# Level-zero attention weights from row products on VectorE instead of tiled matmuls, and tile products kept together on TensorE

## The chip, the cores and the metric

The kernel runs on one core of one Trainium2 chip. The metric is device time in microseconds from launch to the last store, taken as the median over repeated executions. Five engines work side by side, each through its own queue in order: TensorE (matmuls, in the profile PE, with its weight loads as PEld), VectorE (DVE), ScalarE (ACT), GpSimd (POOL) and SyncE (SP, which here only starts transfers). They wait for each other through semaphores.

## The reference

An RWKV-6 attention block feeds an MLP-mixer block. All data is float32 (the four mixer weights are float64 on input and are converted by the kernel itself).

```python
# attention, B, H, S, D = 4, 8, 768, 48
for t in range(S):
    cur = einsum('bhd,bhe->bhde', u[None] * k[t], v[t])
    y[t] = einsum('bhd,bhde->bhe', r[t], state + cur)
    state = w[t][..., None] * state + einsum('bhd,bhe->bhde', k[t], v[t])
# mixer on x = y as (B, S, 384)
xt = x.transpose(0, 2, 1)
h = maximum(xt @ w_tok1, 0) @ w_tok2            # 768 -> 256 -> 768 tokens
uu = x + h.transpose(0, 2, 1)
out = uu + maximum(uu @ w_ch1, 0) @ w_ch2       # 384 -> 1536 -> 384 channels
```

Written without the loop, token t takes from an earlier token s the value v[s] with the weight sum over d of r[t,d] k[s,d] times the product of w over the tokens between them. Its own value has the weight sum over d of r[t,d] u[d] k[t,d]. Between neighbours (s = t-1) no w lies, and the weight is the plain dot product of r[t] and k[t-1].

## The kernel before

**Units.** The work on attention is cut into 12 units of 256 tokens (`NU`), three to a batch (`UB`), each of two chunks of 128 tokens (`UC`), each of two blocks of 64 (`T`). For a unit, r and k lie transposed: features of a pair of heads on the partitions, tokens along the row. Three sets of buffers (`rs`, `ks`, `ws`, `weights_at`) go round.

**Levels.** `levels(i)` fills unit i's 64 by 64 weight matrices in `weights_at` by doubling. At level l, blocks of 2^l tokens are joined: `gram(l)` (L256, and L250 for the last) forms products of k with the r of the neighbouring block on TensorE, in tiles of 64 by 64 or 32 by 32; `join(l)` (L288 to L290) then multiplies k, r and the running products of w on VectorE so that the next level can use them; `pick(l)` (L272 on VectorE, L267 and L280 on ScalarE) copies the wanted entries from PSUM into `weights_at` under a mask. Level 0 is apart. `begin` has ScalarE copy r and k into `rp` and `kp` with every second token multiplied by u (L217, L221). `gram0` (L233) multiplies these in 32 tile products for each unit, and `pick0` (L239) takes own-token and next-token entries.

**Posts.** `post(i)` is what turns the weights into outputs: `tokens` transposes k on TensorE (L323, copied out by ScalarE L324), `carry` forms the k-v products (L333), `update` the states on VectorE (L347, L350), `before` multiplies r by the carried state (L370) and `within` the weights by v (L383). Those three matmul groups use 64 by 64 tiles. Then unit i+3's r, k, w and v are requested on SP's queue.

**Mixing.** `mixing(bt)` is the mixer for one batch: `hidden` (L421), `back` (L428, and an addition on VectorE, L430), transposes (L440), `up` (L448, copied out by L450 on ScalarE), and `down`, in the form `quarters`: seven products (L482) on sums and differences made by VectorE (L474 to L477 and L492 to L520). These matmuls use the whole 128 by 128 array.

**Order.** Beside the mixing of batch bt stand the posts of batch bt+1, and beside post(i) the levels of unit i+1 (`beside`). `woven` merges the two lists by the costs written in them. Below that, the tile framework's scheduler sets the final order of each engine's queue, so the queues aren't simply the order of the calls; it also inserts the waits. PSUM has two `gram` buffers, one pair `a` used in turn by kv_ps and y_ps, and two `m` buffers for mixing; for batches after the first, the transposes of k use `m` too. The last batch's mixing has no attention beside it. The first batch's attention, and the conversion of the mixer weights on VectorE, stand at the start, before any mixing can fill TensorE.

Of the kernel before, what the change touches and what calls it, by code (L numbers as in the profile page):

```python
# [10 lines left out]
f32 = mybir.dt.float32  # L11
# [9 lines left out]
T = 64  # L21
# [33 lines left out]
def rwkv6_then_mixer(  # L55
    ctx: ExitStack,
    tc: tile.TileContext,
    rkw: bass.AP,
    v: bass.AP,
    u: bass.AP,  # L60
    w_tok1: bass.AP,
    w_tok2: bass.AP,
    w_ch1: bass.AP,
# [13 lines left out]

    nc = tc.nc
    pe, dve, act, pool, sp = nc.tensor, nc.vector, nc.scalar, nc.gpsimd, nc.sync

    const = ctx.enter_context(tc.tile_pool(name="const", bufs=1))
    wts = ctx.enter_context(tc.tile_pool(name="wts", bufs=1))
# [16 lines left out]
    def load_rkw(i):  # L99
        if i >= NU:  # L100
            return
        for n, t in enumerate((rs[i % 3], ks[i % 3], ws[i % 3])):
            for rows in (slice(0, 128),) if i < 3 else (slice(0, D), slice(P, P + D)):
                sp.dma_start(t[rows], rkw[i, n, rows, :])
# [7 lines left out]

    u_col = const.tile([128, A], f32, name="u_col")
    act.dma_start(u_col, u)
    load_rkw(0)
    load_rkw(1)

# [3 lines left out]
    for l in range(4):  # L121
        b = 1 << l
        m = const.tile([128, 64 // b, 2 if l == 0 else b], f32, name=f"mask{l}")
        pool.memset(m, 1.0)
        pool.affine_select(out=m, in_=m, compare_op=ALU.is_ge, fill=0.0, base=0,
                           pattern=[[-2 * b, 64 // b], [0, m.shape[2]]], channel_multiplier=1)
        pool.affine_select(out=m, in_=m, compare_op=ALU.is_ge, fill=0.0, base=b - 1,
                           pattern=[[2 * b, 64 // b], [1 if l == 0 else 0, m.shape[2]]], channel_multiplier=-1)
        n, x = (T, 1) if l == 0 else (32, UC * A)
        m8 = const.tile([128, x, n], u8, name=f"mask8_{l}")  # L130
        flat = m.rearrange("p n b -> p (n b)")
        for j in range(2):
            dve.tensor_copy(m8[ts(j, T)], flat[ts(j, T), ts(j, n)].unsqueeze(1).to_broadcast([T, x, n]))
        masks.append(m8)
# [62 lines left out]
    def levels(i):  # L197
# [7 lines left out]
        def begin():  # L205
            decay = apool.tile([128, COLS // 2], f32, name="decay")
            L["w"] = apool.tile([128, UC, A, 2], f32, name="w_chunk", bufs=4)
            pool.memset(L["w"], 0.0)
            products.extend([w_, decay, w_[:, :COLS // 4], decay[:, :COLS // 8], w_[:, :COLS // 16],
                             decay[:, :COLS // 32], L["w"].rearrange("p c a j -> p (c a j)")])  # L210

            rp = L["rp"] = apool.tile([128, COLS], f32, name="rp")
            kp = L["kp"] = apool.tile([128, COLS], f32, name="kp", bufs=1)
            both = [(t.rearrange("p (n two) -> p n two", two=2)[:ROWS], x.rearrange("p (n two) -> p n two", two=2)[:ROWS], o)
                    for t, x, o in ((rp, r_, 1), (kp, k_, 0))]
            for t, x, o in both:
                act.copy(t[:, :, o], x[:, :, o])  # L217
            for t, x, o in both:
                t, x = (e[:, :, 1 - o].rearrange("p (c a n) -> p c a n", c=UC, a=A) for e in (t, x))
                for a in range(A):  # L220
                    act.mul(t[:, :, a, :], x[:, :, a, :], u_col[:ROWS, a:a + 1])  # L221
# [78 lines left out]
            join(l, products[l], products[l + 1])  # L300
            pick(l)

        pieces = [(0.1, begin), (1.6, first_block)]
        for l in range(1, LEVELS):
            pieces.append((1.2, lambda l=l: block(l)))
        return pieces

    def post(i):
        bt, half = divmod(i, UB)
# [3 lines left out]
        def tokens():  # L313
            if half == 0:
                xs[bt] = xpool.tile([128, C, DM], f32, name="x")
            L = live[i]
            L["kT"] = apool.tile([128, UC, A, 128], f32, name="kT", bufs=1)
            if bt == 0:
                both = ps_g.tile([128, 2, 512], f32, name="gram").rearrange("p c (a t) -> p c a t", a=A)
            for c in range(UC):  # L320
                ps = both[:, c] if bt == 0 else ps_m.tile([128, A, 128], f32, name="kT_ps", tag="m")
                for a in range(A):
                    pe.transpose(ps[:, a, :], k_[:, ts(c * A + a, 128)], ident)  # L323
                act.copy(L["kT"][:, c], ps)  # L324
# [207 lines left out]
        downs = [first if (bt, s) == (0, 0) else quarters(s) for s in range(S // SEG)]  # L532
        return hiddens, turned, ups, downs

    def beside(after, ahead):

        tokens, carry, update, before, within, *loads = after
        begin, first, *rest = ahead

        def one(*pieces):  # L540
            return (sum(c for c, _ in pieces), lambda: emit(pieces))

        return [begin, tokens, one(carry, first), update, one(before, rest[0]), one(within, rest[1]), *loads, *rest[2:]]


    hiddens, turned, ups, downs = mixing(0)
# [16 lines left out]
    for bt in range(B):  # L563
# [11 lines left out]
                pieces += ups[s] + downs[s]  # L575
        n = (bt + 1) * UB
        if n < NU:
            att = levels(n) if bt == 0 else []
            for i in range(n, n + UB):
                att += beside(post(i), levels(i + 1)) if i + 1 < NU else post(i)  # L580
            emit(woven(att, pieces))
        else:
            emit(pieces)
# [29 lines left out]
```

## Time and profile before

| | us |
|---|---|
| median of 9 runs | 617.14 (616.83 to 619.69) |
| the profiled execution | 618.18 |
| its span, first to last instruction | 616.4 |
| TensorE matmuls busy | 589.0 |
| TensorE weight loads busy | 500.7 |
| VectorE busy | 341.5 |
| ScalarE busy | 201.6 |
| tile products of level 0 (L233), all 12 units | 22.5 busy, 768 matmuls |

Each float32 matmul of the program stands in the profile as two passes, so 384 products of L233 are 768 entries; transposes are one pass. In the chain of waits, an entry is the time between an instruction and the next on the path, and so the cost of a matmul in a stream; the duration in the list of groups is the latency of one matmul, which overlaps the next. The profile can be cut where the batches' mixing begins, at the first `hidden` matmul of each batch. There are an opening (to 134 us), a stage with the rest of batch 0's mixing (to 235.5), one with batch 1's (to 374), one with batch 2's (to 508), and a last one with batch 3's alone.

### The profile page before, as it was taken

The page shows a single profiled execution, that of the slowest core. Times are in us where ns is not written, and L with a number is a line of the kernel's source. Part 1 is how long each engine was busy: PE and PEld are TensorE (multiplying, and loading weights), DVE is VectorE, ACT ScalarE, POOL GpSimd, SP SyncE. Part 2 cuts the span into 40 slices and gives each one's busy share as a digit, 9 for nine tenths or more (in the row PEclk, how much of TensorE's full clock was granted, in tenths as well). Part 3 has the DMA queues.
Part 4 walks back from the last instruction along what each step waited for, and adds up shares of the span by engine and source line. Part 5 has one row for each costly group of instructions (what it writes and reads, how often), then busy time and mean ns, then how long its engine had stood idle before and what let it go on. Part 6 is the DMA issues. An engine that isn't in the chain of part 4 may idle for free.

```text
span 616.4 us, 19870 instructions
## 1 busy us (share of the span) xinstructions
PE 589.0 (96%) x8980; PEld 500.7 (81%) x8980; DVE 341.5 (55%) x743; ACT 201.6 (33%) x500; POOL 7.2 (1%) x32
## 2 busy tenths in 40 slices
PE   3879789999999999999999999999999999999997
PEld 2867567876888896789899896789899895898987
DVE  5879889998676783536464372616244341040403
ACT  7054555530444433433232422332211411302020
POOL 4000000000000000000000000000000000000000
PEclk9999779999999999999999999999999999999999
DMA  9235555620232112011112100000000000000000
GB/s 347 108 80 190 174 177 163 213 73 27 56 105 79 54 56 79 28 53 28 54 28 79 27 29 27 2 2 3 27 2 28 2 15 14 0 6 21 25 2 26
DMA packets 19380, 38.63 MB, mean 63 GB/s; under 512 B 2112, under 2 KB 12864, under 8 KB 19296
## 3 DMA queue, kind: packets, MB, share of 16 engines
q1 hardware_dynamic: 19152, 37.36, 19.0%
q8 instruction: 70, 1.15, 0.8%
q14 instruction: 14, 0.11, 0.1%
q10 hardware_dynamic: 144, 0.00, 0.0%
HBM read 32.64 MB, written 4.72 MB: 61 GB/s over the span
## 4 chain that ended last, share of the span: by engine, by line
PE 88%; DVE 6%; ACT 2%; DMA 2%; issue 2%; SPq 0%; DVEq 0%; ACTq 0%
PE z_ps L448 29%; PE q_ps L482 25%; PE gram L256 8%; PE h_ps L421 6%; PE h_ps L428 5%; PE h_ps L458 3%; PE kv_ps L333 2%; PE y_ps L383 2%; PE gram L233 2%; PE y_ps L370 2%; PE kT_ps L323 1%; DMA scratch<-in_w_ch_dram 1%; PE gram L250 1%; PE xT_ps L440 1%; DMA w<-in_rkw_dram 1%
## 5 line engine op out<-in xcount | busy, mean ns | idle before, releaser
L448 PE MATMUL z_ps<-xT,wch 128*128 128x256 f32 x864 | 195.9, 382 | 0.1
L448 PEld LDWEIGHTS z_ps<-xT,wch 128*128 128x128 f32 x864 | 161.1, 190 | 22.6 <-ACT z L450 1.0
L450 ACT ACTIVATE z<-z_ps 128x256 f32<-128x256 f32 x144 | 55.1, 382 | 156.6 <-PE z_ps L448 142.1
L482 PE MATMUL q_ps<-wch,z 128*128 128x192 f32 x528 | 93.7, 329 | 0.0
L482 PEld LDWEIGHTS q_ps<-wch,z 128*128 128x128 f32 x528 | 86.3, 190 | 1.3
L482 PE MATMUL q_ps<-scratch,z 128*128 128x192 f32 x396 | 71.1, 330 | 0.0
L256 PEld LDWEIGHTS gram<-r,k 48*64 48x64 f32 x3072 | 60.5, 156 | 11.6 <-issue 5.9
L256 PE MATMUL gram<-r,k 48*64 48x32 f32 x3072 | 65.6, 237 | 3.8 <-DVE at L272 1.9
L482 PEld LDWEIGHTS q_ps<-scratch,z 128*128 128x128 f32 x396 | 64.3, 190 | 0.9 <-ACT kT L324 0.2
L288 DVE TENSOR_TENSOR k<-k,decay 112x512 f32<-112x512 f32 x36 | 24.8, 690 | 49.1 <-PE gram L256 37.0
L474 DVE TENSOR_TENSOR z<-z 128x768 f32<-128x768 f32 x11 | 10.5, 957 | 63.2 <-ACT z L450 63.1
L288 DVE TENSOR_TENSOR k<-k,w 112x512 f32<-112x512 f32 x36 | 24.8, 690 | 36.7 <-PE gram L256 31.5
L421 PE MATMUL h_ps<-x,wtok 128*128 128x384 f32 x96 | 38.9, 557 | 1.7 <-ACT x L389 1.6
L350 DVE SCALAR_TENSOR_TENSOR state<-state,w_chunk,kv_ps 128x48 f32<-128x48 f32 x160 | 30.7, 256 | 17.5 <-PE kv_ps L333 17.5
L428 PE MATMUL h_ps<-h,wtok 128*128 128x384 f32 x96 | 35.5, 494 | 0.1
L233 PE MATMUL gram<-rp,kp 48*64 48x64 f32 x768 | 22.5, 248 | 10.7 <-ACT kp L221 7.9
L272 DVE COPY_PREDICATED at<-mask,gram 128x512 f32<-128x512 uint8 x36 | 32.3, 897 | 0.0
L421 PEld LDWEIGHTS h_ps<-x,wtok 128*128 128x128 f32 x96 | 19.9, 218 | 14.1 <-issue 2.9
L233 PEld LDWEIGHTS gram<-rp,kp 48*64 48x64 f32 x768 | 18.4, 154 | 15.3 <-ACT kp L221 10.3
L280 ACT COPY at<-gram 16x256 f32<-16x256 f32 x48 | 17.4, 364 | 37.2 <-PE gram L256 35.2
L430 DVE TENSOR_TENSOR x<-x,h_ps 128x384 f32<-128x384 f32 x24 | 13.3, 554 | 27.4 <-PE h_ps L428 27.0
L289 DVE TENSOR_TENSOR r<-r,w 112x512 f32<-112x512 f32 x36 | 24.6, 685 | 3.6 <-ACT rp L217 3.6
(80 smaller groups left out, 552.4 us busy)
## 6 DMA issues: line engine op xcount, KB each, us to landing
scratch<-in_w_ch_dram SPq DMA_DIRECT2D x10, 512.0 KB, 4.5
vt<-in_v_dram SPq DMA_DIRECT2D x12, 384.0 KB, 3.7
out_dram<-o SPq DMA_DIRECT2D x24, 192.0 KB, 1.9
x<-in_w_ch_dram SPq DMA_DIRECT2D x8, 512.0 KB, 4.5
w<-in_rkw_dram SPq DMA_DIRECT2D x18, 192.0 KB, 3.3
k<-in_rkw_dram SPq DMA_DIRECT2D x18, 192.0 KB, 3.2
r<-in_rkw_dram SPq DMA_DIRECT2D x18, 192.0 KB, 3.5
scratch<-in_w_tok_dram SPq DMA_DIRECT2D x4, 512.0 KB, 9.1
```

The lines of the kernel that those rows point to most:

```text
L233: pe.matmul(g[cols, q, ts(a, T)], L["kp"][rows, tokens], L["rp"][rows, tokens], start=True, stop=True)
L256: fours(lambda q, j, rows, cols: pe.matmul(g[cols, q, ts(ca, 32)], k_[rows, ds(ca * 128 + j * T, T)], right[rows, ts(2 * ca + j, 32 // b), ...
L272: dve.copy_predicated(out=dst, data=g.rearrange("p q (m b) -> p q m b", b=b), mask=masks[l].rearrange("p x t -> p (x t)").rearrange("p (m ...
L288: dve.tensor_mul(left, left, wv[:, :, 1].unsqueeze(2).to_broadcast([ROWS, n, b]))
L289: dve.tensor_mul(right, right, wv[:, :, 0].unsqueeze(2).to_broadcast([ROWS, n, b]))
L350: dve.scalar_tensor_tensor(new[:, a], state[bt, g][:, a], L["w"][:, c, a, j:j + 1], got[:, a], op0=ALU.mult, op1=ALU.add)
L421: pe.matmul(sums[i], wtok1[:, c, ts(i, 128)], xs[bt][:, c, :], start=(c == 0), stop=(c == C - 1))
L428: pe.matmul(ps, wtok2[:, i, ts(c, 128)], h1[:, i, :], start=(i == 0), stop=(i == DTOK // 128 - 1))
L448: pe.matmul(ps, wch1[:, m, ts(jt, 128)], xT[:, m, ts(s, SEG)], start=(m == 0), stop=(m == DM // 128 - 1))
L450: act.activation(zs[s][:, jt, :], ps, AF.Relu)
L458: pe.matmul(ps, zs[0][:, jt, ts(n, 128)], wch2[:, jt, :], start=(jt == 0), stop=(jt == NJ - 1))
L482: pe.matmul(ps, a[:, j, :], b[:, j, :], start=(j == 0), stop=(j == HJ - 1))
```

## The change

- For units 3 to 11 `gram0`, `pick0` and the copies into `rp` and `kp` are gone; `begin` does `join(0)` instead.
- Their level-0 weights come from VectorE (`nearest`). r, the r of the following token, and k are loaded once more with tokens on the partitions (`load_near`: four more transfers for each unit on SP's queue, two of 384 KB and two of 192 KB). `row` multiplies them for one chunk of 128 tokens and sums over each head's 48 features; `place` writes the sums under the mask into `weights_at`.
- In `late`, the first unit's `nearest` is ordered behind VectorE's and SP's newest instructions at that point; the order of the others is left to the scheduler.
- `beside` orders the products of unit i+1's level 1, 2 and 3 directly behind the tile products of `carry`, `before` and `within` of unit i, as one run in tiles.
- The transposes of k always use one `gram` buffer, and `begin` gets a larger cost in the weaving, so that mixing stands between the last gram and the transposes.

```diff
@@ levels(i), begin
+            if i >= UB:
+                join(0, products[0], products[1])
+                return
...
-        pieces = [(0.1, begin), (1.6, first_block)]
+        pieces = [(0.1, begin)] + ([(1.6, first_block)] if i < UB else [])
...
+    def load_near(i):
+        if i >= NU:
+            return
+        L = near_by[i] = [apool.tile([128, COLS], f32, name="kp", bufs=1)]
+        for c in range(UC):
+            t = apool.tile([128, COLS], f32, name="rp")
+            sp.dma_start(t[:, :2 * DM].rearrange("p (two e) -> p two e", two=2), near[i - UB, c, :, :2, :])
+            sp.dma_start(L[0][:, ts(c, DM)], near[i - UB, c, :, 2, :])
+            L.append(t)
...
+        def row(c):
+            k, t = near_by[i][0][:, ts(c, DM)], near_by[i][1 + c]
+            rr = t[:, :2 * DM].rearrange("p (two e) -> p two e", two=2)
+            if c == 0:
+                sums.append(apool.tile([128, UC, 2 * H], f32, name="sums"))
+            dve.tensor_mul(rr, rr, k.unsqueeze(1).to_broadcast([128, 2, DM]))
+            dve.tensor_mul(rr[:, 0], rr[:, 0], u_rows)
+            dve.tensor_reduce(out=sums[0][:, c], in_=t[:, :2 * DM].rearrange("p (h e) -> p h e", e=D),
+                              axis=mybir.AxisListType.X, op=ALU.add)
+        def place():
...
+            for q in range(2):
+                dve.tensor_copy(v[:, q, :, :, 0], own[:, q])
+                dve.scalar_tensor_tensor(v[:, q, :, :, 1], own[:, q], odd, later[:, q], op0=ALU.mult, op1=ALU.add)
+            dve.copy_predicated(
+                out=weights_at[i % 3].rearrange("p q x (m two) -> p (q x) m two", two=2),
+                data=two.rearrange("p q x two -> p (q x) two").unsqueeze(2).to_broadcast([128, 2 * UC * A, T // 2, 2]),
+                mask=masks[0].rearrange("p x (m two) -> p x m two", two=2).to_broadcast([128, 2 * UC * A, T // 2, 2]))
+        return [(0.3, lambda: row(0)), (0.3, lambda: row(1)), (0.2, lambda: (place(), load_near(i + 1)))]
...
@@ post(i), tokens
-            if bt == 0:
-                both = ps_g.tile([128, 2, 512], f32, name="gram").rearrange("p c (a t) -> p c a t", a=A)
+            both = ps_g.tile([128, 2, 512], f32, name="gram").rearrange("p c (a t) -> p c a t", a=A)
             for c in range(UC):
-                ps = both[:, c] if bt == 0 else ps_m.tile([128, A, 128], f32, name="kT_ps", tag="m")
+                ps = both[:, c]
...
@@ beside
+        def both(f, g):
+            behind = products(f)[-1].name
+            for ins in products(g):
+                tc.add_manual_dep(ins, behind, no_sync, reason="products in tiles together")
         def one(*pieces):
-            return (sum(c for c, _ in pieces), lambda: emit(pieces))
-        return [begin, tokens, one(carry, first), update, one(before, rest[0]), one(within, rest[1]), *loads, *rest[2:]]
+            return (sum(c for c, _ in pieces), lambda: both(*(f for _, f in pieces)))
+        return [(1.0, begin[1]), tokens, one(carry, rest[0]), update, one(before, rest[1]), row0, one(within, rest[2]),
+                *loads, row1, *rest[3:], place]
...
@@ main loop, batch 0
+                marks = {e: newest(e) for e in (sp, dve)}
+                late(marks, lambda: (sp.dma_start(u_rows, u_all), load_near(n)))
+                att += levels(n) + [(c, lambda f=f: late(marks, f)) for c, f in nearest(n)]
```

`near` and `u_all` are new arrays laid out by the host from r, k and u, copies without arithmetic; `odd` is a column with one on the odd partitions, made once from the level-0 mask.

## The prediction, made before the changed kernel ran

> **What bounds the kernel now.** I read the busy table by stage first, cut where each batch's mixing begins (start:end, length, then PE, PEld, DVE and ACT busy).
>
> ```profile
> 0.00:133.96 133.96, 110.99 (x2059) 90.16 (x2060) 115.89 (x255) 65.84 (x153) 6.66 (x27) 0.95 0.54 175
> 133.96:235.50 101.54, 100.53 (x2303) 83.26 (x2302) 77.00 (x163) 37.20 (x97) 0.34 (x3) 1.00 0.23 65
> 235.50:373.95 138.45, 138.45 (x2217) 119.51 (x2218) 69.67 (x154) 45.45 (x118) 0.22 (x2) 1.00 0.14 41
> 373.95:507.83 133.88, 133.78 (x1871) 115.40 (x1871) 54.00 (x127) 34.51 (x86) 0.00 (x0) 1.00 0.03 11
> 507.83:616.40 108.57, 105.23 (x534) 92.42 (x533) 24.90 (x46) 18.65 (x47) 0.00 (x0) 1.00 0.04 13
> ```
>
> From 134 us on TensorE has no idle time to speak of. VectorE has 24.5 us free in the second row (101.5 - 77.0), 69 and 80 us in the next two. The opening is VectorE's and the transfers'. Busy doesn't prove full speed, so I took prices from the chain of waits (start, length, what), where matmuls stand at the rate at which they follow each other:
>
> ```profile
> 440.70 1.08 PE kv_ps L333 x64
> 441.78 0.94 PE gram L233 x58
> 442.72 9.26 PE z_ps L448 x42
> 507.83 7.74 PE h_ps L421 x24
> 554.68 15.54 PE z_ps L448 x72
> 599.41 13.66 PE q_ps L482 x84
> ```
>
> A pass of L448 is 15.54 / 72 = 0.216 us, of L482 0.163, of a 384-wide product 0.323. A tile pass is about 0.0145, reached when a tile block follows another. A block of tiles behind whole-array work costs some 0.14 more (1.08 against 0.94), and the first whole-array block behind tiles 0.2 more (9.26 against 42 x 0.216 = 9.06). Transposes of k take 0.135, of x 0.11, the last gram's 32 by 32 tiles 0.009, all from the same view.
>
> With these prices and the order of the instructions, the four stages sum to 99.0, 137.2, 132.5 and 105.0 us; the trace has 101.5, 138.5, 133.9 and 105.2. So TensorE's own work is all but 5 us of the last 479, and that work is what a change must cut. The view of waits agrees; from 134 to 508 us it has one entry for matmuls:
>
> ```profile
> PE kT_ps L323 <- DVE k L288: 0.8, 2, 0.5
> ```
>
> [...] The 768-wide product measures 0.957, or 0.87 from start to start.
>
> **What the change takes away.** 32 products, 64 passes, for each of nine units. 512 of the 576 passes lie behind 134 us: 512 x 0.0145 = 7.4 us. The order of the instructions moves one more gram block (0.9) from the second stage into the opening, where TensorE has time. Tile products kept together, and transposes no longer mixed with level-0 products, cut the changes between tiles and whole array behind 134 us from 70 each way to 46: with the prices of each kind, 22.3 to 15.3 us, or 7.0. Together 15.3. By stage the sums are 89.9, 134.8, 128.9 and 105.0: less by 9.1, 2.4, 3.6 and 0.
>
> ScalarE loses 9 x (2 x 0.67 + 8 x 0.405) = 41 us of copies. It is 37 of 101 us busy in the fullest stage, so this is worth nothing directly. It can shorten the wait of the transposes for buffers; the 2.5 us between 99.0 and 101.5 bound that.
>
> **What it adds.** Nearest rows on VectorE (line, tiles, shape, count, busy and mean ns, idle before):
>
> ```profile
> L239 DVE COPY_PREDICATED at<-mask,gram 128x512 f32<-128x512 uint8 x24 | 17.2, 725 | 1.3 <-PE gram L233 1.2
> L474 DVE TENSOR_TENSOR z<-z 128x768 f32<-128x768 f32 x11 | 10.5, 957 | 63.2 <-ACT z L450 63.1
> L515 DVE TENSOR_TENSOR o<-o,z 128x384 f32<-128x384 f32 x11 | 6.1, 558 | 0.3
> ```
>
> Successive operations overlap by some 0.08 us (L288 takes 0.69 and the next starts 0.61 later), so I count from start to start. Each chunk: a 768-wide product 0.87, a 384-wide one 0.48, a reduce of 768. The reduce isn't in the trace: [...] 0.96 if like L474 without overlap; I take 0.86. Each unit also has four small operations, 0.1 each (L290 on 16 elements is 0.17 without overlap). The masked copy of 1024 is not there either. [...] the masked copy of level 1, whose runs are two elements long, takes twice as long as those of longer runs:
>
> ```profile
> 194.93 1.30 DVE L272 COPY_PREDICATED at<-mask,gram 128x512 f32<-128x512 uint8 x1
> 199.74 0.71 DVE L272 COPY_PREDICATED at<-mask,gram 128x512 f32<-128x512 uint8 x1
> ```
>
> The new copy reads 512 pairs, which at that price is 2 x 1.08 = 2.2. Its destination and mask run on without gaps, so I take 1.4. A unit costs 2 x 2.21 + 0.4 + 1.4 = 6.2, less two L239 copies, 1.2: about 5 us net, 45 over nine units.
>
> Spread evenly this hides under the 173 us that VectorE has free. It isn't spread evenly. In the order of the changed kernel, `late` holds back only the first unit; all others depend on their loads alone, and VectorE's queue in the second stage holds 12 of the 18 wide products, 11 narrow, 10 reduces, 10 pairs of small operations and 3 of 9 masked copies ahead of the operation that frees the PSUM buffer for batch 1's first matmul. That is 10.4 + 5.3 + 8.6 + 2.0 + 4.2 = 30.5 us. What else stands there, at start-to-start prices, is 64.6 (the 77.0 of before without six L239 copies, without one level of joins that moves into the opening, and without the last rows of the stage). VectorE starts 0.9 us after TensorE here, so even without a pause it reaches that operation at 0.9 + 95.1 = 96.0, where TensorE would be at 89.9. **In this stage VectorE becomes the bound.** It won't run without a pause, since joins still wait for grams; I add 2 us, an estimate between the 24.5 it was idle and none. The stage takes 98.0: 3.5 us less, not 9.1.
>
> What is late next: 13.2 us of VectorE work stand between that operation and the end of batch 1's first addition to x, for which the first transpose of x waits. TensorE has about 14 us of its own before it (the 12 products of `hidden`, two passes each, 0.645, the transposes of k, a tile run, the first products of `back`). I take 0.5 us. The third stage then gains 2.4 - 0.5 = 1.9. VectorE is about half busy from there, with 4 wide products left, and the fourth gains 3.6.
>
> **Transfers.** Four more issues a unit on SP, 0.38 us each, two of 384 KB (v's, the same size, land in 3.7 us) and two of 192 (3.3). Space for the next pair of rows is freed by a reduce, and between a reduce and the product that reuses its buffer lie 6.5 to 11 us of VectorE work: 0.4 + 3.7 fits, with 2.4 us to spare at the tightest. I take 1 us in all, and 5 or more as the bad case below. DMA engines are a quarter busy.
>
> **Opening.** Two L239 copies (1.2) leave VectorE, one level's join and pick (2.5) come in, where it idles 0.8 us for a transfer; the transposes ahead of SP's wait at 78 us come earlier. I take -0.3, from -1 to +1.
>
> **Sum.** -0.3 - 3.5 - 1.9 - 3.6 + 1.0 = -8.3 against the profiled span of 616.4 us (618.18 with what lies around it). The median of runs is 617.14, 1 us below that execution; taking the difference to it gives **609.0 us**.
>
> **Rivals.**
>
> 1. *TensorE stays the bound throughout*: the whole 15.3 arrives, near 603. For it speaks that TensorE was the bound everywhere. Against it stands the sum of VectorE's queue: [...].
> 2. *The unseen operations are dear*: masked copy 2.2, reduce 0.96. Then the second stage takes 3 x 0.8 + 10 x 0.1 = 3.4 more and 1 more in the next: 613.4.
> 3. *Slower: VectorE stands in line for late row loads.* SP takes its queue in order, and loads of r stand in it until `before` has read r:
>
> ```profile
> SPq L104 <- PE y_ps L370: 15.2, 2, 7.8
> ```
>
> That is 15.2 us in two waits in the second stage alone. A row load behind such a wait misses its 2.4 us, its product stops VectorE's queue with the joins behind it, and as VectorE is the bound there each us counts. It turns the gain into a loss from 8.3 us in all, 0.7 for each of 12 products. At 1 us each: 621. Against it: the rows run units ahead of need, and the loads go out between the waits.
>
> That the change doesn't do what it says (tile runs torn apart again by the scheduler) is ruled out by the order, where the 46 changes stand.
>
> **How the numbers follow.** Chances: the forecast 0.50 (its own range 605 to 613), rival 1 0.09, rival 2 0.22, rival 3 0.19. Leaving out half of rival 1 and most of rival 3's tail, the range is 604 to 619. A change of 0.2%, 1.2 us, is about what can be told from none. Faster: 0.50 + 0.09 + 0.16 of rival 2 = 0.75. The same: 0.05 of rival 2, 0.04 of rival 3. Slower: 0.01 and 0.15.
>
> **What will show it.** The second stage near 98 us with VectorE over 90 busy, and TensorE waiting there for VectorE some 6 to 9 us; 136.5 and 130 in the next two; the last unchanged. Runs of 128 tile passes, and no L233 group beyond the first three units. Prices of the reduce and the wide masked copy decide between the forecast and rival 2, idle time of the row products for transfers rival 3. The prediction fails if VectorE reads rows slower than the 768-wide row says, or if TensorE's switch prices aren't what the tile runs save.

## The result

The changed kernel takes 612.12 us, the median of 16 runs (607.82 to 615.18), against 617.0 for the kernel before beside it. The ratio is 0.992 (95% interval 0.9904 to 0.9937): faster by 0.8%. The forecast was 609.0 with a range from 604 to 619. The profiled execution took 612.79 us, with a span of 611.0; the span of before was 616.4.

The busy table of the changed kernel by stage, cut as in the prediction (start:end, length, PE, PEld, DVE, ACT and POOL busy, then the mean granted TensorE clock, the share of the DMA engines and GB/s):

```profile
0.00:132.90 132.90, 109.19 (x2059) 88.78 (x2060) 115.27 (x256) 56.65 (x128) 6.66 (x27) 0.88 0.58 187
132.90:237.40 104.50, 96.55 (x1946) 80.54 (x1945) 98.43 (x209) 23.94 (x61) 0.34 (x3) 0.95 0.41 117
237.40:373.13 135.73, 135.57 (x2128) 117.57 (x2128) 87.07 (x188) 36.98 (x93) 0.22 (x2) 1.00 0.23 69
373.13:502.51 129.38, 129.38 (x1743) 112.39 (x1743) 54.75 (x129) 32.48 (x81) 0.00 (x0) 1.00 0.03 11
502.51:611.00 108.49, 105.24 (x535) 92.52 (x533) 24.91 (x46) 18.60 (x47) 0.00 (x0) 1.00 0.04 13
```

Only the later cuts stand at a batch's first `hidden` product; the first stands at batch 0's first product of `down` (L458 before, L533 now).

| stage | before | after | change | forecast |
|---|---|---|---|---|
| opening | 133.96 | 132.90 | -1.1 | -0.3 |
| second | 101.54 | 104.50 | **+3.0** | -3.5, and +1.0 for transfers |
| third | 138.45 | 135.73 | -2.7 | -1.9 |
| fourth | 133.88 | 129.38 | -4.5 | -3.6 |
| last | 108.57 | 108.49 | -0.1 | 0 |
| sum | 616.40 | 611.00 | -5.4 | -8.3 |

So one stage went the other way. In the second row VectorE is busy 98.4 of 104.5 us, TensorE 96.6, and the clock column reads 0.95, where before it read 1.00. Neither engine is without a pause, and TensorE was not at full speed.

TensorE's longest waits from the second stage to the end of the fourth (line waited for: us in all, times, longest); the one entry of before was 0.8 us:

```profile
PE gram L289 <- DVE r L322: 3.4, 4, 1.2
PE gram L289 <- issue: 3.2, 2, 2.1
PE y_ps L445 <- DVE state L425: 0.9, 2, 0.7
```

TensorE now waits for the joins of VectorE (L322), and twice for nothing that the profile can name ("issue"). The chain of the fourth stage shows what the change did for TensorE where nothing disturbs it: `carry` and a gram block follow each other with one change to tiles, and the same rates hold as before.

```profile
439.73 1.08 PE kv_ps L408 x64
440.81 0.93 PE gram L289 x63
```

The new operations, which the trace of before couldn't price (groups: out<-in, shape, count, busy and mean ns, idle before):

```profile
L362 DVE TENSOR_TENSOR rp<-rp,kp 128x768 f32<-128x768 f32 x18 | 17.1, 952 | 1.1 <-DMA rp<-in_near_dram 1.1
L364 DVE TENSOR_REDUCE sums<-rp 128x16 f32<-128x768 f32 x18 | 17.0, 946 | 0.1
L375 DVE COPY_PREDICATED at<-mask,two 128x1024 f32<-128x1024 uint8 x9 | 11.8, 1310 | 1.0 <-ACT at L300 0.9
L363 DVE TENSOR_TENSOR rp<-rp,u_rows 128x384 f32<-128x384 f32 x18 | 9.9, 552 | 0.1
```

The reduce runs like the product of its width, 0.946 us against 0.952. The masked copy of 1024 takes 1.31 us, near the 1.4 taken and far from the 2.2 of rival 2. In the whole kernel the row products waited 1.1 us in all for their own loads.

The second stage's chain, in the middle (start, length, what), names two things that the forecast had not placed:

```profile
195.86 0.21 SPq L128
...
196.12 4.05 DMA r<-in_rkw_dram
...
200.26 0.69 DVE r L322
...
202.30 1.13 PE gram L289 x62
203.43 1.11 issue
...
204.96 3.71 PE z_ps L523 x8
```

A load of r, not of a row, came late: its two halves were issued at 195.69 and 196.12, VectorE waited 1.4 us for them, to 200.26, and TensorE got its gram at 202.30. Then TensorE stopped in the middle of its gram passes for 1.11 us with nothing to wait for. And 8 passes of L523 took 3.71 us, where 8 x 0.216 = 1.73 is their price.

### The profile page after: what moved, and what is told of

Same layout as the page of the kernel before. It is cut to its first block, busy times and chain, and to the rows that moved or that the text cites. A ratio compares the mean times of both kernels' runs of the same rounds, so it can differ in the third digit from the quotient of the medians.

```text
span 611.0 us, 18750 instructions
## 1 busy us (share of the span) xinstructions
PE 575.9 (94%) x8404; PEld 491.8 (80%) x8404; DVE 380.4 (62%) x826; ACT 168.6 (28%) x410; POOL 7.2 (1%) x32
## 3 DMA queue, kind: packets, MB, share of 16 engines
q8 instruction: 66, 1.08, 0.8%
## 4 chain that ended last, share of the span: by engine, by line
PE 74%; DVE 18%; issue 4%; ACT 2%; DMA 2%; SPq 0%; DVEq 0%; ACTq 0%
PE z_ps L523 24%; PE q_ps L557 23%; PE gram L289 6%; PE h_ps L496 6%; PE h_ps L503 5%; DVE r L322 2%; PE y_ps L458 2%; DVE k L321 2%; PE kv_ps L408 2%; PE y_ps L445 2%; DVE state L425 1%; PE gram L398 1%; DVE wch L205 1%; DVE at L305 1%; DVE rp L362 1%
## 5 line engine op out<-in xcount | busy, mean ns | idle before, releaser
L523 PE MATMUL z_ps<-xT,wch 128*128 128x256 f32 x864 | 197.9, 385 | 0.1
L523 PEld LDWEIGHTS z_ps<-xT,wch 128*128 128x128 f32 x864 | 162.6, 192 | 22.4 <-ACT z L525 1.4
L557 PE MATMUL q_ps<-wch,z 128*128 128x192 f32 x528 | 96.0, 333 | 0.0
L557 PEld LDWEIGHTS q_ps<-wch,z 128*128 128x128 f32 x528 | 88.1, 193 | 1.7 <-DVE o L579 0.3
L557 PE MATMUL q_ps<-scratch,z 128*128 128x192 f32 x396 | 70.3, 329 | 0.1
L557 PEld LDWEIGHTS q_ps<-scratch,z 128*128 128x128 f32 x396 | 64.4, 190 | 0.7 <-issue 0.3
L549 DVE TENSOR_TENSOR z<-z 128x768 f32<-128x768 f32 x11 | 10.5, 957 | 61.8 <-ACT z L525 61.8
L321 DVE TENSOR_TENSOR k<-k,decay 112x512 f32<-112x512 f32 x36 | 24.8, 688 | 31.3 <-PE gram L289 18.7
L321 DVE TENSOR_TENSOR k<-k,w 112x512 f32<-112x512 f32 x36 | 24.8, 689 | 30.2 <-PE gram L289 25.1
L322 DVE TENSOR_TENSOR r<-r,w 112x512 f32<-112x512 f32 x36 | 24.7, 686 | 4.7 <-DMA r<-in_rkw_dram 4.7
L322 DVE TENSOR_TENSOR r<-r,decay 112x512 f32<-112x512 f32 x36 | 24.6, 685 | 0.0
L503 PEld LDWEIGHTS h_ps<-h,wtok 128*128 128x128 f32 x96 | 16.9, 193 | 9.7 <-ACT h L498 2.5
```

Source lines behind the costliest of these rows:

```text
L321: dve.tensor_mul(left, left, wv[:, :, 1].unsqueeze(2).to_broadcast([ROWS, n, b]))
L322: dve.tensor_mul(right, right, wv[:, :, 0].unsqueeze(2).to_broadcast([ROWS, n, b]))
L503: pe.matmul(ps, wtok2[:, i, ts(c, 128)], h1[:, i, :], start=(i == 0), stop=(i == DTOK // 128 - 1))
L523: pe.matmul(ps, wch1[:, m, ts(jt, 128)], xT[:, m, ts(s, SEG)], start=(m == 0), stop=(m == DM // 128 - 1))
L557: pe.matmul(ps, a[:, j, :], b[:, j, :], start=(j == 0), stop=(j == HJ - 1))
```

## The experiments

Three theories stood against each other at first. **V**: VectorE's row operations, which only their loads hold back, run ahead and stand in VectorE's queue before the joins that TensorE waits for. **T**: TensorE's lower clock is the loss. **S**: the late loads of r are. All edits are to the changed kernel unless another is named.

| kernel | whole us (runs) | ratio to before, 95% | second stage | DVE busy in it | clock in it |
|---|---|---|---|---|---|
| after | 612.12 (16) | 0.992, 0.9904 to 0.9937 | 104.5 | 98.4 | 0.95 |
| e1_spread | 606.79 (5) | 0.9836, 0.981 to 0.9862 | 95.7 | 89.9 | 1.00 |
| e2_no_rows | 601.6 (5) | 0.9765, 0.9735 to 0.9796 | 93.9 | 75.4 | 1.00 |
| e3_together_only | 613.67 (12) | 0.9949, 0.9933 to 0.9965 | 100.3 | 75.0 | 1.00 |
| e4_near_only | 614.35 (20) | 0.9954, 0.9935 to 0.9972 | 102.7 | 102.4 | 0.99 |
| e5_loads_only | 611.47 (6) | 0.9912, 0.9877 to 0.9947 | 102.5 | 76.9 | 0.97 |
| e6_spread_apart | 604.47 (5) | 0.9802, 0.9777 to 0.9827 | 93.7 | 89.4 | 1.00 |
| e7_spread_pool | 610.98 (6) | 0.9903, 0.9867 to 0.994 | 100.7 | 87.7 | 0.98 |
| e8_short_loads | 607.07 (5) | 0.984, 0.9809 to 0.9871 | 98.4 | 97.5 | 1.00 |
| e9_loads_held | 604.02 (4) | 0.98, 0.9772 to 0.9827 | 95.7 | 76.0 | 1.00 |

Each ratio sets a kernel against executions of before that were taken with it. e2, e5, e8 and e9 leave out a part of the computation, as told below. The second stage is cut at the same two matmuls in all. The openings lie between 131.5 and 135.5 us and hide or add a little of it, so a length is read beside the whole time. In e2, e5, e8 and e9 the order puts one gram block of 64 passes (0.9 us) into this stage that the changed kernel, e1, e6 and e7 have in the third.

### Rows held at their place (e1)

```diff
-        row0, row1, place = nearest(i + 1)
+        row0, row1, place = ((c, lambda f=f: late({dve: newest(dve)}, f)) for c, f in nearest(i + 1))
```

Every unit's row operations now stay behind the operation that was VectorE's newest where their piece stands, not only the first unit's.

> Every row, sum and copy of the new VectorE work stays behind VectorE's newest instruction at its place in the list, so it no longer runs units ahead. TensorE's order stays nearly the same (its sums by stage: 89.9, 134.8, 128.9, 105.0 us). VectorE's work up to the operation that frees batch 1's first PSUM buffer falls from 94.5 to 85.8 us, below TensorE's 89.9. Theory V (VectorE's queue is what made the second stage long): that stage goes from 105.3 us to 92 to 96, and the whole to about 602 (600 to 605). Theory T (TensorE's granted clock, 0.80 in one stretch of that stage, made it long): the stage stays at 102 or more, the whole at 610 to 613. Theory S (late loads of r): the stage stays above 100 with VectorE waiting for transfers.

Measured 606.79 us, second stage 95.7. Nothing was taken away: the same operations, loads and tile runs, 8.8 us less in that stage. Only the order differs. The stage lies where V had put it and the clock in it was 1.00; the whole is 1.8 us above V's range, and the opening took 134.9, 2.0 more than in the changed kernel. At this point I took V for settled, and T and S for refuted: T had said 610 to 613, S a stage above 100. That was too quick, as e5 shows: holding the products also holds the loads that wait for their buffers, so e1 changes two things at once.

### Rows left out, and each half of the change alone (e2, e3, e4)

e2 leaves out the loads, products and sums of the rows, with constant weights in their place:

```diff
...
-            dve.tensor_mul(rr, rr, k.unsqueeze(1).to_broadcast([128, 2, DM]))
-            dve.tensor_mul(rr[:, 0], rr[:, 0], u_rows)
-            dve.tensor_reduce(out=sums[0][:, c], ...)
+                sums.append(flat_sums)
...
-        return [..., (0.2, lambda: (place(), load_near(i + 1)))]
+        return [..., (0.2, place)]
...
-                late(marks, lambda: (sp.dma_start(u_rows, u_all), load_near(n)))
```

> Leaves out part of the computation: the new loads, the row products and the sums; the level-0 weights of units 3 to 11 are placed from a constant. What is left of the change on VectorE is the small operations and the masked copy. TensorE's work and order as in the changed kernel. Theory V: the second stage is TensorE's again, 91 to 95 us, and the whole 599 to 603; this is the ceiling of what the change could give. Theory T: still 610 or so, with the clock low in the second stage. Theory S can't be told from V here, since loads and rows are both gone.

601.6 us, second stage 93.9: the ceiling, and close to the 603 of rival 1. Rows cost the changed kernel 10.5 us of the whole, nearly all of it in the second stage (104.5 - 93.9 = 10.6).

e3 keeps level 0 on TensorE for all units and takes only the other half: tile products together, transposes of k in the gram buffer.

```diff
-            if i >= UB:
-                join(0, products[0], products[1])
-                return
...
-        return [(1.0, begin[1]), tokens, one(carry, rest[0]), update, one(before, rest[1]), row0, one(within, rest[2]),
-                *loads, row1, *rest[3:], place]
+        return [(1.0, begin[1]), tokens, one(carry, first), update, one(before, rest[0]), one(within, rest[1]),
+                *loads, *rest[2:]]
...
```

> Level 0 stays on TensorE for all units, as before the change; tile products are ordered behind one another and the transposes of k use a gram buffer with mixing ahead of them. TensorE's sums by stage: 95.7, 137.7, 131.5, 105.0 us against 99.0, 137.2, 132.5, 105.0 before, all of it from fewer changes between tiles and whole array (109 against 139). If the price of such changes is right (0.14 to 0.2 us each): 3.8 us less than before, 613 to 614, second stage about 98. If they cost nothing by themselves: 617. Theory T adds: if longer runs of tile products lower the clock, the clock is below that of before, and the time is no better.

613.67 us, as expected: 15 of 70 changes to tiles and back fall away, which by the sums of the expectation is 3.8 us; the medians differ by 3.1 (0.0051 x 617). The second stage is 100.3 in the profiled execution, not the 98 expected, but that execution (615.64) was the slowest of the twelve.

e4 is the other half: rows on VectorE, tile products not kept together, transposes of k as before.

```diff
-            return (sum(c for c, _ in pieces), lambda: both(*(f for _, f in pieces)))
+            return (sum(c for c, _ in pieces), lambda: emit(pieces))
...
-            both = ps_g.tile([128, 2, 512], f32, name="gram").rearrange("p c (a t) -> p c a t", a=A)
+            if bt == 0:
+                both = ps_g.tile([128, 2, 512], f32, name="gram").rearrange("p c (a t) -> p c a t", a=A)
...
-                ps = both[:, c]
+                ps = both[:, c] if bt == 0 else ps_m.tile([128, A, 128], f32, name="kT_ps", tag="m")
...
-        return [(1.0, begin[1]), tokens,
+        return [begin, tokens,
...
```

> Row products on VectorE as in the changed kernel, but no order between tile products, transposes of k in the mixing's PSUM buffers and the weaving costs of before. TensorE's sums by stage: 95.1, 133.1, 130.0, 105.0 us. VectorE's work up to batch 1's first free buffer 94.5 us, as in the changed kernel. Theory V: the second stage is as long as in the changed kernel, 103 to 106 us, since VectorE's queue sets it whatever TensorE saves; the whole 611 to 614. Theory T (tile runs lower the clock): the clock is back to 0.985 or more and the stage under 100, the whole 605 to 609.

614.35 us, second stage 102.7 with VectorE busy in 102.4 of it: VectorE is the bound here without a doubt; the whole is 0.35 us above V's range. Its chain also names a load of a row's k, 2.51 us from 231.81 on, but VectorE had other work in that time and was idle for only 0.14 us before the product that reads it.

### Loads without work, and work without loads (e5, e8, e9)

e5 keeps the loads and replaces the three wide operations by one small product, so it has next to none of the work that V blames:

```diff
...
-            dve.tensor_mul(rr, rr, k.unsqueeze(1).to_broadcast([128, 2, DM]))
-            dve.tensor_mul(rr[:, 0], rr[:, 0], u_rows)
-            dve.tensor_reduce(out=sums[0][:, c], ...)
+            dve.tensor_mul(sums[0][:, c], t[:, :2 * H], k[:, :2 * H])
```

> The changed kernel with its row loads where they were, but the three wide operations of a row replaced by one small product of 16 elements that reads both loaded tiles (so the weights beside the diagonal are wrong: left out are the row products and the sums). Theory V (what the second stage lost is VectorE's queue, the transfers cost nothing): as the kernel without loads, second stage 93.5 to 95.5 us, whole 601 to 604 us, no clock below 0.98 in that stage and no gap over 1 us inside a run of tile passes that the kernel without loads did not have. Theory L (the row loads, through memory traffic or through SP's queue in front of the loads of r, cost the 3 to 4 us that VectorE's busy time does not explain): second stage 97 to 99, whole 605 to 607.

I missed badly: 611.47 us, second stage 102.5, with VectorE busy for 77 of it. It is worse than theory L itself expected. Without wide work between them the small products reach the front of VectorE's queue before their loads have landed, and the joins stand behind them. Its chain:

```profile
147.61 4.20 DMA kp<-in_near_dram
...
151.90 0.17 DVE sums L361
152.08 0.28 DVE k L321
...
152.60 0.70 DVE r L322
...
153.43 0.82 PE gram L283 x44
```

```profile
DVE r L322 <- DMA r<-in_rkw_dram: 4.7, 2, 3.2
DVE sums L361 <- DMA kp<-in_near_dram: 1.9, 2, 1.7
```

A load of a row takes 4.2 us and VectorE stands idle for the last 1.7 of them before a product of 0.17 us; the joins at L321 and L322 stand behind it and TensorE, 1.8 us without work, behind these. That is the mechanism of rival 3, in a kernel where it has room. Loads of r were waited for longer, 4.7 us in two waits. But most of the 8.6 us over e2 are of another kind: two stretches at half clock (12 passes of L553 in 3.38 us and 12 in 3.82, where 12 x 0.163 = 1.96 is their price: 3.3 us) and pauses of TensorE that the profile names nothing for, 4.6 us against 2.1 in e2. The two sections below are about these.

e9 is e5 with the small products held at their place as in e1:

> e5_loads_only (full row loads, one small product of each row instead of the three wide operations; the row sums are left out) with every unit's small products held behind VectorE's newest operation at their place, so that the loads that wait for their buffers go out at that pace too. Theory E (loads cost only when they go out early and in a burst, with VectorE's queue standing behind them): second stage 93.5 to 96, TensorE clock 0.99 or more in it, whole 601 to 604.5. Theory N (the number of bytes or issues is what costs): second stage over 99, whole 606 or more, as e5_loads_only.

604.02 us, second stage 95.7, clock 1.00: theory E. The same bytes and issues cost 6.8 us less there, 7.4 in the medians, when they and their products are held; 2.4 us over e2 are left. Held products don't stand in line for their rows either, so e9 doesn't tell that part from the loads going out early.

e8 goes the other way. VectorE's row operations keep their number, sizes and place, and read the constant row of u; the loads stay four to a unit and shrink to 8 of 128 partitions. The tile for k goes, and with it the waits of its loads for that buffer:

```diff
-        L = near_by[i] = [apool.tile([128, COLS], f32, name="kp", bufs=1)]
+        L = near_by[i] = [None]
...
-            sp.dma_start(t[:, :2 * DM].rearrange("p (two e) -> p two e", two=2), near[i - UB, c, :, :2, :])
-            sp.dma_start(L[0][:, ts(c, DM)], near[i - UB, c, :, 2, :])
+            sp.dma_start(t[:8, :DM], near[i - UB, c, :8, 0, :])
+            sp.dma_start(t[:8, DM:2 * DM], near[i - UB, c, :8, 1, :])
...
-            k, t = near_by[i][0][:, ts(c, DM)], near_by[i][1 + c]
+            k, t = u_rows, near_by[i][1 + c]
...
-            dve.tensor_mul(rr, rr, k.unsqueeze(1).to_broadcast([128, 2, DM]))
+            dve.tensor_mul(rr, k.unsqueeze(1).to_broadcast([128, 2, DM]), k.unsqueeze(1).to_broadcast([128, 2, DM]))
```

> The changed kernel with VectorE's row operations all in the order they have there, but fed from the constant row of u; the four loads of a unit are kept and shortened to 8 of 128 partitions (left out: the products of the true rows, so the weights beside the diagonal are wrong). Theory V (VectorE's row work standing ahead of the joins is the loss, and the half-speed stretches of TensorE follow the waits that it makes): second stage 98 to 104 us, VectorE busy over 96 of it, whole 607 to 612. Theory L (the row loads are the loss: they make the loads of r late, and the waits for r bring the half-speed stretches): second stage 94 to 96.5, whole 601 to 605.

607.07 us. Its second stage, and that of e9 (columns as in the first table):

```profile
133.90:232.30 98.40, 92.71 (x2010) 77.37 (x2008) 97.45 (x211) 23.99 (x61) 0.33 (x3) 1.00 0.23 64
```

```profile
133.30:229.00 95.70, 92.18 (x2009) 77.71 (x2008) 75.99 (x181) 24.00 (x61) 0.33 (x3) 1.00 0.37 106
```

With VectorE's work alone the stage is 98.4 us and VectorE has 1 us free in it. This is what V says and what the forecast said (98.0). The whole is at V's lowest value, because no half-speed stretch followed here. So the second stage of the changed kernel comes apart as: 93.9 without rows, 4.5 for VectorE's work in that order (98.4), 6.1 for the full loads on top (104.5). By the medians of the whole it is 601.6, 5.5 and 5.0. In this order V explains about half. The two don't simply add up: with the loads taken first, e5 stands at 102.5 and the wide work adds only 2.0, though e5 has waits of its own.

### What follows a wait: TensorE's clock (s1, s2)

The granted clock is either 1.0 or 0.5 in the profiles of before and of the changed kernel, and it changes on a grid of 3.41 us: the stretches at half clock up to 600 us are 3.41, 6.83 or 10.24 us long. Two pairs of windows of the changed kernel, cut on that grid:

```profile
200.63:204.04 3.41, 1.61 (x65) 1.13 (x63) 3.41 (x8) 0.38 (x1) 0.00 (x0) 1.00 0.57 208
204.04:210.87 6.83, 6.33 (x78) 4.84 (x79) 4.59 (x7) 3.13 (x9) 0.00 (x0) 0.50 0.47 139
227.93:231.35 3.42, 1.35 (x25) 1.20 (x18) 3.42 (x6) 0.86 (x2) 0.00 (x0) 1.00 0.40 122
231.35:234.76 3.41, 3.41 (x23) 2.97 (x21) 1.95 (x5) 0.00 (x0) 0.00 (x0) 0.50 0.39 120
```

In the first window TensorE worked 1.61 us: it was waiting for the joins behind the late r and then through the 1.11 us of pause. In the third it lost 2.07 us in a pause of the same kind. After each the clock stands at 0.50. In the second stages of all kernels of the table, five such windows had TensorE busy for 1.35 to 1.63 us, and half speed followed each; of fourteen with 1.92 to 2.59 us it followed one (2.41, in e4). The kernel before, e3 and e6 have no window below 2.6 us there.

Busy time alone doesn't decide, though. In the openings of the two kernels, from the first record of the clock on (63.1 us before, 43.6 in the changed kernel), half speed followed each of the five windows at full clock with less than 2.6 us of work: two of before with 1.15 and 1.60 us of work (66.54, 80.19), and three of the changed kernel with 2.11, 1.89 and 2.02 (43.61, 60.68, 77.74), where 56 of 64 passes, all 104 and all 122 are tile passes. Here is the last of them, and what came after it:

```profile
77.74:81.16 3.42, 2.02 (x122) 1.85 (x115) 3.42 (x16) 0.12 (x1) 0.11 (x1) 1.00 0.91 268
81.16:91.40 10.24, 9.41 (x137) 6.58 (x130) 8.54 (x18) 3.48 (x8) 0.00 (x0) 0.50 0.59 165
```

Yet a window of e1 with 127 tile passes and 2.16 us, at 221.69, kept its clock. So half speed followed each of the eight windows with 1.63 us or less that these openings, the second stages and s2 below show; after 1.89 to 2.59 us it went both ways, after 2.64 us or more it never came, and what decides between is open.

The stretches cost, by the chain: 8 passes at 3.71 against 1.73, 2 at 1.15 against 0.43, and 14 of L557 at 4.00 against 14 x 0.163 = 2.28, or 4.4 us. With the pauses, 3.2 us against 1.7 in e8, that is 5.9 of the 6.1. The first stretch, 2.7 us of the 4.4, follows the late load of r and a pause; the second follows a pause alone. So T and S, which e1 seemed to refute, each name a part of the loss.

To see whether a wait alone brings this, I put one wait into the kernel before, in its last stage, where nothing else happens. Three (in s2 twelve) more operations, which leave the values as they are, stand on VectorE between a ReLU and the product that reads it:

```diff
                 act.activation(h1[:, i, :], sums.pop(i), AF.Relu)
+                if bt == B - 1 and i == DTOK // 128 - 1:
+                    for _ in range(3):
+                        dve.tensor_tensor(out=h1[:, i, :], in0=h1[:, i, :], in1=h1[:, i, :], op=ALU.max)
```

> The kernel before, with three products more on VectorE (maximum of h1 with itself, 384 wide, about 0.5 us each) between the last ReLU of the last batch's token mixing and the products that read it: one wait of TensorE of about 1.5 us in the last stage. Theory H (TensorE's clock is halved for 3.41 us after a 3.41 us window in which TensorE was busy for less than about half): no such window, last stage 1.4 to 1.9 us over the 108.57 of before, clock 1.00 in all of it. Rival (no wait is followed by a lower clock): the same.

> As s1_stall_3 with twelve such operations: one wait of 5.8 to 6.2 us. Theory H: at least one window of 3.41 us falls into the wait, so a stretch of 3.41 or 6.83 us at half clock follows, and the last stage is 1.7 or 3.4 us longer than the wait alone makes it: 7.3 to 9.6 us over 108.57, the clock 0.5 in that stretch. Rival (the half-speed stretches have another cause than TensorE's waits): 5.8 to 6.4 us over 108.57, clock 1.00.

There is one execution of each. The last stage takes 109.92 us with three (1.35 over before) and 116.98 with twelve (8.41 over). Around the long wait:

```profile
515.00:518.43 3.43, 0.36 (x2) 0.00 (x0) 3.24 (x6) 0.00 (x0) 0.00 (x0) 1.00 0.00 0
...
521.50:525.25 3.75, 3.69 (x8) 2.32 (x9) 1.12 (x3) 0.08 (x1) 0.00 (x0) 0.50 0.00 0
```

With three the clock is 1.00 throughout. With twelve, the clock is halved when the first idle window ends, while TensorE is still waiting, and stays so for 3.75 us of work. Twelve operations took 7.08 us and three 1.74, so nine more are 5.3 us; the stage grew by 7.1. The other 1.7 is close to half of the 3.75 us at half clock. Theory H; the short wait cost a little less than expected, 1.35 for 1.4 to 1.9. For it H and its rival said the same, so s2 alone decides: after a window with 0.36 us of work the clock stood at 0.50, and the first four passes of L431 took 2.93 us against 1.56 with three operations. That a half-filled window does the same rests on the windows above.

### Tile runs, and GpSimd (e6, e7)

The second pause of the changed kernel, 2.07 us, lies inside a run of 128 tile passes, 64 of `y_ps` and 64 of a gram. e6 is e1 without the code that keeps such passes together:

```diff
-            return (sum(c for c, _ in pieces), lambda: both(*(f for _, f in pieces)))
+            return (sum(c for c, _ in pieces), lambda: emit(pieces))
```

> The kernel with every unit's rows held behind VectorE's newest operation at their place (e1_spread), but its tile products no longer kept together. From the order of the instructions TensorE then changes 50 times each way between tiles and whole-array work behind 134 us instead of 46, which at 0.14 and 0.2 us is 1.4 us more work. Theory V: where VectorE no longer sets the second stage, that is what it costs: 607 to 609 us, 1 to 2 over e1_spread. Theory G (a run of 128 tile passes costs more than it saves, as the gaps of 1 to 2 us near its end in the trace suggest): at or below e1_spread, 604.5 to 606.8, and no such gaps.

604.47 us, 2.3 below e1 and the best kernel that computes the whole. The time is that of theory G, and the pauses are gone; its reason is not what G says. Here are the same passes in e8, which has the runs, and in e6, where the scheduler happens to leave this one together:

```profile
221.69 0.71 issue
222.40 0.65 PE q_ps L557 x3
223.05 1.08 PE y_ps L458 x64
224.13 0.91 PE gram L289 x61
225.03 0.98 issue
226.01 0.30 PE gram L289 x3
```

```profile
222.06 1.08 PE y_ps L458 x64
223.13 0.92 PE gram L289 x64
```

A run of 128 is no slower in itself: e6's takes 2.0 us without a stop. The pause stands at a fixed place instead. In the changed kernel, e1, e2, e5, e7, e8 and e9 it comes after 61 of the same 64 gram passes, for 0.8 to 2.1 us. In e2, e5, e7, e8 and e9 another, of 0.4 to 1.0 us, comes 3 + 64 + 61 = 128 passes ahead of it. What stands near it in the trace is a queue. The changed kernel's list of DMA queues has one for instructions, with 66 packets of 16 KB, 1.08 MB in all. From 134 to 500 us, 49 of these packets start in before and 45 in the changed kernel, one for 256 and for 257 matmul and load entries of TensorE on the mean. The changed kernel's two pauses end 1.34 and 1.27 us after such a packet has ended (at 203.20 and 229.00), and only 5% of that time lies 1.1 to 1.5 us behind one. The packet of the 1.11 us pause started 1.32 us ahead of it, that of the 2.07 us pause 0.15 us ahead. No run here changed these packets. That they make the pauses is a guess of mine and was not shown; whether the early loads made the later packet late stays open too. What e6 shows is that another order of the same work has no such pause, and that four changes to tiles and back more, 1.4 us by the prediction's prices, cost less than this.

e7 moves the product with u to GpSimd, on top of e1:

```diff
-            dve.tensor_mul(rr[:, 0], rr[:, 0], u_rows)
+            pool.tensor_mul(rr[:, 0], rr[:, 0], u_rows)
```

> e1_spread with the product with u (384 wide, 18 of them, 9.9 us of VectorE in all) on GpSimd. Theory V (VectorE still sets a little of e1_spread's second stage): VectorE's work up to the release falls from 85.8 to 82.4 us, second stage 94 to 95.7, whole 605 to 607. Rival P (GpSimd is slow at it and VectorE waits for it between product and sum, or is slowed while both read): row sums wait over 1 us for GpSimd each, second stage over 97, whole 608 or more.

610.98 us, rival P in its time and stage. The product takes 1.26 us on GpSimd on the mean, 0.55 on VectorE, and the first one in the chain 3.63. In the second stage the sums behind it waited 5.8 us in six waits, the longest 1.2, so a little under 1 us each, and a window with TensorE busy for 1.39 us was followed by half speed. VectorE's own product and sum took 0.95 us as before: it was not slowed, it waited.

## Why the prediction was right, and where it wasn't

**TensorE's sums.** Right. In the third stage -2.7 against -1.9, in the fourth -4.5 against -3.6: somewhat better than forecast, by the same steps. e3, with 15 of the 24 changes each way, agrees with the prices of 0.14 and 0.2 us (3.1 measured, 3.8 by the sums). What the step left out is that the new order brings pauses of its own: e6, with 50 changes each way, beats e1 with 46.

**VectorE becomes the bound in the second stage.** Right, and right in size. The queue sum 95.1 and 0.9 for the start, with pauses, gave 98.0; e8 measures 98.4, with VectorE busy in 97.5 of it. Without the loads of full size the forecast of this stage would have stood.

**The unseen operations.** Reduce 0.95 us busy, 0.86 from start to start (0.86 taken, an estimate), masked copy 1.31 (1.4 taken, an estimate as well). Rival 2 fell.

**Transfers: the step that failed.** The sum had 1 us in all and 5 or more as the bad case; measured are 6.1 in the second stage, 5.0 by the medians (e8 against the changed kernel), with what the clock and the pauses made of them. The place was wrong as well. I looked for the product that waits for its own row, as rival 3 put it, with 2.4 us to spare at the tightest: such waits are 1.1 us. What came late was a load of r. SP takes its queue in order, as the two views below show, and the row loads in it wait for VectorE's buffers: SP's longest entry in that stage is the row load of L348 waiting for the product at L362: 25.0 us in four waits, the longest 13.1.

Before, loads of r stood only behind their own buffers; now a row load that VectorE hasn't made room for stands ahead of what is queued later. SP's queue around the late load, in the kernel before and then in the changed one:

```profile
193.51 1.15 SPq L104 DMA_DIRECT2D r<-in_rkw_dram  x2
```

```profile
193.70 1.89 SPq L348 DMA_DIRECT2D kp<-in_near_dram  x2
195.69 0.85 SPq L128 DMA_DIRECT2D r<-in_rkw_dram  x2
```

The last reader of r, a run of `before`'s products, ended at 193.45 and at 193.43. Before, r's load went out 0.06 us later; in the changed kernel two row loads stood first, waited for L362 to 193.70 and kept SP to 195.59, and r went out 2.3 us late. In e1, e5, e8 and e9 the same load goes out within 0.1 us of its last reader. So it was this line that made it late. That loads held at their place cost far less, 2.4 us by the medians (e9 against e2), and loads of 8 partitions spare the 5.0, the runs show; how the loss divides between late loads of r, the pauses and the clock is read from the traces, and no run takes these apart.

**What was missing.** The prediction took TensorE's price per pass as fixed. It wrote that busy doesn't prove full speed, read rates from the chain, and did not ask what happens to the rate once TensorE has to wait. In the changed kernel a pause of 2.07 us, in a window that had only 1.35 us of work in it, was followed by 3.41 us at half clock, and 14 passes of L557 took 4.00 us where 2.28 is their price.

**The sign and the range.** Faster, inside the range. The rivals' places: 603 for TensorE as the bound throughout is what e6 nearly reaches with the rows held; rival 3's mechanism, VectorE in line for a row, shows in e5, and VectorE stood idle 1.1 us for it in the changed kernel. That the sum came within 3 us is partly luck: with the 1.0 for transfers the second stage was to get 2.5 us shorter and got 3.0 longer, while the other four stages together saved 2.6 us more than forecast. Two slips in the working change little: 617.14 - 8.3 is 608.8, not 609.0, and the stages' 9.1, 2.4 and 3.6 make 15.1, not 15.3.

## What to carry to other kernels

When a change takes the last bound off TensorE in a stage, the waits that appear there can cost more than their length, so cut the trace on the clock's windows. Here the five windows of the second stages with 1.35 to 1.63 us of work (changed kernel, e5, e7) were each followed by 3.41 or 6.83 us at half clock, half of which I count as lost; with 1.89 to 2.59 us of work it went both ways. Work moved to an engine with time to spare has to be held at its place in that engine's queue, and its loads with it; here that was one line, worth 5.3 us (e1). An experiment that holds work back also holds its loads back: take away each alone before the cause is named. And a load's entry in the chain is not the time that was waited for it: in e4 it stood there with 2.51 us and VectorE was idle for 0.14.

## What the runs showed of the hardware

- The half-speed stretches: on a grid of 3.41 us, 3.41 or 6.83 us long in the second stages and there only after windows in which TensorE stood still for 1 us or more (busy for 1.35 to 1.63 or, in e4, 2.41 us); in the opening of before 6.83 us long, twice, in that of the changed kernel 10.24 us, three times. The grid stands 1.69 us behind the span's start in the profile of before and 2.65 us in that of the changed kernel. The changed kernel's times scatter more than e6's (607.8 to 615.2, 603.5 to 605.8); that the grid makes them do so was not shown.
- TensorE's pauses without a releaser, 0.4 to 2.1 us, at the same place in the order of seven kernels and 128 passes apart where there are two. In the changed kernel the two of 1.11 and 2.07 us end 1.34 and 1.27 us behind the end of a 16 KB packet on the instruction queue. After the window with the second (1.35 us of work) the clock stood at 0.50.
- A masked copy of 1024 elements whose data are pairs repeated over 32 positions takes 1.31 us from SBUF; one of 512 from PSUM with runs of two took 1.30, with longer runs 0.71. By element the first is near the longer runs (1.28 ns against 1.39), far from the short ones (2.54).
